# Linear attention and mixture of depths on one core: the first four passes written apart, the order of the later ones changed

## The chip, the core and the metric

One core of a Trainium2 chip. The metric is the device time of one execution in microseconds. The core has five engines with a queue each: PE (TensorE, matmuls and transposes), DVE (VectorE), ACT (ScalarE), POOL (GpSimd) and SP (SyncE, which here only issues DMAs). Each engine takes its instructions in the order in which the kernel writes them, and they wait for one another through semaphores.

## The reference

q, k and v are 8 batches x 8 heads x 576 positions x 64, in float32. With softmax of q over its 64 features and softmax of k over the 576 positions, per head

```
kv  = softmax_seq(k)^T @ v          # 64 x 64
x_h = softmax_feat(q) @ kv          # 576 x 64
```

and the heads side by side make x, 576 x 512 for each batch. Then a mixture of depths: scores are x @ w_gate; the 128 positions with the highest scores of each batch are chosen, and for these alone

```
out[chosen] = x[chosen] + sigmoid(score) * (relu(x[chosen] @ w1) @ w2)   # 512 -> 1024 -> 512
```

Every other row of the output is x.

## The kernel before

A unit is four heads of one batch, so there are 16 units and two to a batch. The kernel's main loop runs over slots `s` = 0 to 19; slot `s` does the attention of unit `s`, prepares unit `s + 1`, and from slot 4 on (`LAG`) also does the MLP of batch `(s - 4) // 2`: its first product (`mlp1`) in the even slots, its second (`mlp2`) in the odd ones, in eight pieces each. Slots 0 to 3 (`EARLY`) have no MLP; filler matmuls (`fill`) stand there instead. The order of all engines' work is written out by hand: what the loop body calls first is first in each engine's queue.

The steps of a unit:
- `load` (L96): k, v and q by two DMAs each on SP's queue, 1.77 MB a unit, into one of three buffers for each (`LD`); a load waits until its buffer has been read.
- `k_exp` (L192) and `q_exp` (L199): exponentials on ScalarE. No maximum is subtracted; a check at the end can start a general version.
- `v_copy` (L202): VectorE copies v beside a column of ones, for the sums of k's softmax.
- `kv_mm` (L212): 40 matmuls of 128 x 64 weights, into a PSUM bank of the pool `tp`. `kv_out` (L221 to L226): reciprocals, the copy of kv into SBUF, and kv times w_gate as one column more.
- `q_t` and `q_t_last` (L235, L244): transposes of exp(q) into `tp` banks; ScalarE (L237) and VectorE (L246) copy them out into `qT`, scaled by the reciprocals of kv.
- `x_mm` (L256): two halves of 40 matmuls of 64 x 64 weights. `x_out` (L269 to L272): VectorE divides by q's sums and writes x and the scores. `x_store` (L277): x goes to the output, on SP's queue.

The steps of a batch, once both units are there: `score`; `score_row` (L305, L308, L310: the scores as a row on every partition, through `tp` banks); five `compare` (L318: each position's rank); `pick` (L338 to L350: a mask of those with ranks below 128, five matmuls on PE that give their indices, and the gather of their rows of x by GpSimd's indirect DMA); `gate`; `turn` (L371, L373: the gathered rows transposed on PE and copied out by ScalarE); `mlp1` (L385, L388), `mlp2` (L395), `finish` (L403, L404: gate and add on VectorE, and the scatter into the output).

PSUM has eight banks: `tp` two, in turn, for q's transposes, kv, score rows and picks; `mm` two, in turn, for fillers, `turn`, `mlp1` and `mlp2`; `x` four, two for each half. A new tile in a bank waits until the one before it there has been read.

In the kernel before, batch 0's `pick` stands in slot 3 and its `turn` in slot 4; in general batch b's pick stands in slot 2b + 3 and its turn at the start of slot 2b + 4:

```
        if chosen is not None:
            pick(chosen)
        if here:
            x_mm(s, 0)
            x_out(s, 0)
```

Of the kernel before, what the change touches and what calls it, by code (L numbers as in the profile page):

```python
# [17 lines left out]
def kernel(  # L18
# [20 lines left out]
    nc = tc.nc  # L39
    B, H, S, D = q.shape  # L40
    DM, F = moe_w1.shape
    P = 128
    R = 5
# [7 lines left out]
    C = D + 2  # L51
# [3 lines left out]
    UP = 2.0 ** 24  # L55
    TINY = 2.0 ** -126
    NV = 5
    WARM = 24
    assert S == 64 * (R + N2) and D == 64 and DM == H * D and DM == 512 and H % 4 == 0
    assert 1 < capacity < S and KF == 8 and NQ == 2  # L60
    assert B * S <= 32 * 256
# [20 lines left out]
    NU = len(units)  # L82
# [115 lines left out]
        qr = raw["q"][u % LD].rearrange("p (i h) r d -> p i r h d", i=2)  # L198
        nc.scalar.activation(out=st["qe", u][:, i], in_=qr[:, i], func=AF.Exp)  # L199

    def v_copy(u):
        nc.vector.tensor_copy(out=v_ones[u % 2][:, :, :, :D], in_=raw["v"][u % LD])  # L202

    def kv_mm(u):

# [19 lines left out]
        nc.vector.tensor_mul(prod, kv[:, :, :D], wg[:, qd])  # L225
        nc.vector.reduce_sum(out=kw[:, :, D + 1], in_=prod, axis=AX.X)  # L226

    def q_t(u, i):

        if i == 0:  # L230
            st["qT", u] = at.tile([P, 2, R, P], F32, tag="qT", name="qT")
        qe = st["qe", u]
        t_ps = bank("tp", 2)
        for r in range(N2):
            nc.tensor.transpose(out=t_ps[:, r * P:(r + 1) * P],  # L235
                                in_=qe[:, i, r].rearrange("p h d -> p (h d)"), identity=ident)
        nc.scalar.activation(out=st["qT", u][:, i, :N2].rearrange("p r c -> p (r c)"), in_=t_ps,  # L237
                             func=AF.Copy, scale=krec[:, u, i:i + 1])
# [10 lines left out]
    def x_mm(u, i):  # L249


        qT = st["qT", u] if i == 0 else st.pop(("qT", u))
        x = ps.tile([P, 2, 512], F32, tag="x", name="x", bufs=2)
        for r in range(R):
            for h, c in ((0, 0), (1, 1), (0, 1), (1, 0)):
                nc.tensor.matmul(out=x[part(c), h, r * C:(r + 1) * C], lhsT=qT[part(h), i, r, part(c)],  # L256
                                 rhs=kv_w[u % 2][part(h), i], start=True, stop=True)
        st["x", u] = x

    xs, sr = {}, {}  # L260

    def x_out(u, i):
        b, qd = units[u]
        if qd == 0 and i == 0:
            xs[b] = xp.tile([P, R, NQ, 2, 2, D], F32, tag="xs", name="xs")
            sr[b] = md.tile([P, NQ * 2, G], F32, tag="sr", name="sr")
        x = st.pop(("x", u))[:, :, :R * C].rearrange("p h (r c) -> p h r c", r=R)
        rec = qrec[:, u, i].rearrange("p (h r) -> p h r", h=2)
        nc.vector.reciprocal(out=rec, in_=x[:, :, :, D])  # L269
        nc.vector.tensor_mul(xs[b][:, :, qd, i].rearrange("p r h d -> p h r d"), x[:, :, :, :D],  # L270
# [248 lines left out]
    v_copy(0)  # L519
    kv_and_exp(0)  # L520
    load(3, "kvq")
    load_w1(0)
    load_w1(1)

    number = None
    for s in range(NU + LAG):

        mlp_b, odd = divmod(s - LAG, 2)
        busy = s >= LAG
        first = busy and odd == 0  # L530
        piece = mlp1 if first else mlp2
        f_next = 0

        def pieces(n):
            nonlocal f_next
            for _ in range(min(n, 8 - f_next) if busy else 0):
                each(piece, mlp_b, f_next)
                f_next += 1

        here = s < NU  # L540
        after = s + 1 < NU
        last = s == NU - 1
        early = s < EARLY
        ends = s // 2 if here and s % 2 == 1 else None
        compared = s // 2 - 1 if s % 2 == 0 and 2 <= s < NU else None
        chosen = (s - 3) // 2 if s % 2 == 1 and 3 <= s < NU else None
        if s == NU:
            chosen = B - 1
        if here:
            q_t(s, 0)  # L550
            q_t_last(s)
        if first:
            each(turn, mlp_b)
        else:
            pieces(1)
        if here:
            q_t(s, 1)
        if early:
            fill(6)
        if compared is not None and early:  # L560
            score_row(compared)
        if after and not early:
            v_copy(s + 1)
        pieces(1)
        if chosen is not None:
            pick(chosen)
        if here:
            x_mm(s, 0)
            x_out(s, 0)
        if compared is not None and not early:  # L570
            score_row(compared)
        if after:
            k_exp(s + 1)
        if compared is not None and early:
            for r in range(R):
                compare(compared, r)
        if after and early:
            v_copy(s + 1)
        pieces(1)
        if here:  # L580
            x_mm(s, 1)
            x_out(s, 1)
            x_store(s)
        if early:
            fill(6)
        if last:
            score(ends)
        pieces(1)
        if after:
            kv_and_exp(s + 1)  # L590
        if early:
            fill(8)
        if s == 0:
            load_w1(2)
            load_w1(3)
        if s + 4 < NU:
            load(s + 4, "kvq")
        if s in (1, 2):
            load_w2(s - 1)
        if compared is not None and not early:  # L600
            for r in range(R):
                compare(compared, r)
        if last:
            score_row(ends)
            for r in range(R):
                compare(ends, r)
        if chosen is not None:
            each(gate, chosen)
        if ends is not None and not last:
            score(ends)  # L610
        pieces(8)
        if busy and odd == 1:
            each(finish, mlp_b)
        if s == NU:
            number = sums_in_range()
# [28 lines left out]
```

## Time and profile before

| | us |
|---|---|
| median of 3 runs | 238.59 (238.51 to 239.07) |
| the profiled execution | 240.16 |
| its span | 238.4 |
| PE busy | 211.9 (89%) |
| DVE busy | 126.7 (53%) |
| ACT busy | 85.9 (36%) |
| POOL busy | 30.8 (13%) |

The rows below come from the profiled execution; its times count from the span's start. PE is the matmuls, PEld the loads of weights, which overlap them. [...] A float32 matmul shows as two instructions, so an `mlp2` piece (one matmul) is "x2" and an `mlp1` piece (four) is "x8". A line of the chain of waits says from when and for how long a piece of work was what the end waited for.

### The profile page before, as it was taken

What the parts mean: (1) busy time and instruction counts of PE and PEld (TensorE: products, weight loads), DVE (VectorE), ACT (ScalarE), POOL (GpSimd) and SP (SyncE); (2) the same over time, 40 slices, a digit from 0 to 9 for tenths busy, and PEclk for the clock granted to TensorE, in tenths of its full rate; (3) what the DMA queues carried; (4) which work ended last, traced back from release to release, by engine and by line L of the source; (5) the groups of instructions that cost most, each with busy time, mean ns of one, the idle gap of its engine ahead of it and who ended that gap; (6) DMA issues with size and microseconds to landing.
All of it is one profiled execution on the core that took longest, in us unless ns stands there. A gap on an engine that the chain in (4) does not pass through costs nothing.

```text
span 238.4 us, 6902 instructions
## 1 busy us (share of the span) xinstructions
PE 211.9 (89%) x2937; PEld 159.4 (67%) x2937; DVE 126.7 (53%) x379; ACT 85.9 (36%) x146; POOL 30.8 (13%) x74
## 2 busy tenths in 40 slices
PE   6977727879999999999999999999999987998980
PEld 2566626769766995599659956896589646947730
DVE  6455385645954495539653774477447666401010
ACT  2456432446333434444435352626163310110200
POOL 5000100120014001300121011201110112101001
PEclk9999986999999999999999999999999998899997
DMA  6999999999958492759485858530413041101001
GB/s 195 314 357 363 388 374 371 376 381 381 381 167 260 179 319 94 242 200 304 138 257 190 258 168 254 206 102 3 143 47 102 1 145 45 44 3 47 1 5 48
DMA packets 39334, 46.79 MB, mean 196 GB/s; under 512 B 2944, under 2 KB 36736, under 8 KB 39296
## 3 DMA queue, kind: packets, MB, share of 16 engines
q1 hardware_dynamic: 36928, 41.36, 51.6%
q0 software_dynamic: 1280, 4.20, 5.2%
q10 hardware_dynamic: 1088, 0.72, 1.1%
q8 instruction: 25, 0.41, 0.7%
q14 instruction: 13, 0.11, 0.1%
HBM read 34.73 MB, written 11.53 MB: 194 GB/s over the span
## 4 chain that ended last, share of the span: by engine, by line
PE 73%; DMA 11%; DVE 5%; ACT 5%; issue 2%; POOL 1%; SPq 0%; POOLq 0%; ACTq 0%
PE mm L385 26%; PE mm L395 23%; DMA q<-in_q_dram 8%; PE x L256 8%; PE tp L212 7%; PE tp L235 5%; DMA xr<-out_dram,idx 3%; ACT qT L237 2%; PE tp L305 2%; DVE junk L318 2%; ACT qe L199 1%; DVE o L403 1%; DVE v_ones L202 1%; PE tp L244 1%; ACT xT L373 0%
## 5 line engine op out<-in xcount | busy, mean ns | idle before, releaser
L385 PE MATMUL mm<-xT,w 128*128 128x128 f32 x512 | 65.3, 284 | 1.6 <-ACT xT L373 1.6
L385 PEld LDWEIGHTS mm<-xT,w 128*128 128x128 f32 x512 | 60.8, 196 | 3.6 <-ACT xT L373 2.4
L395 PE MATMUL mm<-w,hT 128*128 128x512 f32 x128 | 62.1, 607 | 0.0
L318 DVE SCALAR_TENSOR_TENSOR junk<-srow,s,not_before 128x576 bf16<-128x576 f32 x40 | 32.7, 817 | 2.7 <-ACT srow L310 1.5
L395 PEld LDWEIGHTS mm<-w,hT 128*128 128x128 f32 x128 | 21.7, 190 | 16.5 <-issue 15.3
L212 PE MATMUL tp<-v_ones,ke 128*64 128x65 f32 x640 | 23.5, 229 | 9.5 <-DVE qrec L269 8.6
L212 PEld LDWEIGHTS tp<-v_ones,ke 128*64 128x64 f32 x640 | 21.2, 143 | 15.1 <-issue 12.0
L237 ACT ACTIVATE qT<-tp,krec 128x512 f32<-128x512 f32 x32 | 22.0, 687 | 23.9 <-PE tp L235 23.9
L270 DVE TENSOR_TENSOR xs<-x,qrec 128x640 f32<-128x640 f32 x32 | 26.4, 824 | 1.1
L256 PEld LDWEIGHTS x<-kv_w,qT 64*64 64x64 f32 x1280 | 21.5, 133 | 6.7 <-ACT qe L199 3.8
L256 PE MATMUL x<-kv_w,qT 64*64 64x66 f32 x1280 | 25.6, 223 | 0.0
L199 ACT ACTIVATE qe<-q 128x640 f32<-128x640 f32 x32 | 23.6, 736 | 2.7 <-DMA q<-in_q_dram 2.7
L269 DVE RECIPROCAL qrec<-x 128x10 f32<-128x10 f32 x32 | 7.0, 220 | 31.7 <-PE x L256 31.7
L235 PE MATMUL tp<-ident,qe 128*128 128x128 f32 x128 | 19.9, 279 | 2.9 <-ACT qT L237 2.4
L235 PEld LDWEIGHTS tp<-ident,qe 128*128 128x128 f32 x128 | 14.6, 143 | 11.2 <-ACT qT L237 7.9
L350 POOL DMA_INDIRECT xr<-out_dram,idx x8 | 7.9, 992 | 105.3 <-DVE qrec L269 72.6
L403 DVE SCALAR_TENSOR_TENSOR o<-mm,g,xr 128x512 f32<-128x512 f32 x8 | 6.0, 750 | 29.0 <-PE mm L395 29.0
L192 ACT ACTIVATE ke<-k 128x1280 f32<-128x1280 f32 x16 | 20.4, 1272 | 1.8 <-DMA k<-in_k_dram 1.8
L223 ACT COPY kv_w<-tp 128x130 f32<-128x130 f32 x16 | 4.3, 266 | 45.3 <-DVE krec L221 45.3
L388 ACT ACTIVATE hT<-mm 128x512 f32<-128x512 f32 x16 | 9.6, 597 | 29.3 <-PE mm L385 29.3
L404 POOL DMA_INDIRECT out_dram<-o,idx x8 | 11.2, 1397 | 40.4 <-DVE o L403 40.4
L221 DVE RECIPROCAL krec<-tp 128x2 f32<-128x2 f32 x16 | 2.7, 171 | 20.3 <-PE tp L212 20.3
(83 smaller groups left out, 146.9 us busy)
## 6 DMA issues: line engine op xcount, KB each, us to landing
k<-in_k_dram SPq DMA_DIRECT2D x16, 320.0 KB, 5.2
q<-in_q_dram SPq DMA_DIRECT2D x16, 320.0 KB, 6.4
out_dram<-xs SPq DMA_DIRECT2D x16, 320.0 KB, 3.2
v<-in_v_dram SPq DMA_DIRECT2D x15, 320.0 KB, 5.8
k<-in_k_dram SPq DMA_DIRECT2D x16, 256.0 KB, 4.4
q<-in_q_dram SPq DMA_DIRECT2D x16, 256.0 KB, 7.0
out_dram<-xs SPq DMA_DIRECT2D x16, 256.0 KB, 3.7
v<-in_v_dram SPq DMA_DIRECT2D x15, 256.0 KB, 5.3
```

The costliest lines, as they stand in the source:

```text
L192: nc.scalar.activation(out=ke, in_=raw["k"][u % LD], func=AF.Exp)
L199: nc.scalar.activation(out=st["qe", u][:, i], in_=qr[:, i], func=AF.Exp)
L212: nc.tensor.matmul(out=kv[part(h), i], lhsT=ke[:, 2 * i + h, r], rhs=vo[:, 2 * i + h, r], start=(r == 0), stop=(r == N2))
L235: nc.tensor.transpose(out=t_ps[:, r * P:(r + 1) * P], in_=qe[:, i, r].rearrange("p h d -> p (h d)"), identity=ident)
L237: nc.scalar.activation(out=st["qT", u][:, i, :N2].rearrange("p r c -> p (r c)"), in_=t_ps, func=AF.Copy, scale=krec[:, u, i:i + 1])
L256: nc.tensor.matmul(out=x[part(c), h, r * C:(r + 1) * C], lhsT=qT[part(h), i, r, part(c)], rhs=kv_w[u % 2][part(h), i], start=True, stop=True)
L270: nc.vector.tensor_mul(xs[b][:, :, qd, i].rearrange("p r h d -> p h r d"), x[:, :, :, :D], rec.to_broadcast([P, 2, R, D]))
L318: nc.vector.scalar_tensor_tensor(junk, st["srow", b], st["s", b][:, r:r + 1], not_before[:, r], op0=OP.subtract, op1=OP.is_ge, accum_out=s ...
L385: nc.tensor.matmul(out=h_ps[:, f % 4 * m:(f % 4 + 1) * m], lhsT=w1[:, d, f * P:(f + 1) * P], rhs=xT[:, d, :m], start=(d == 0), stop=(d == ...
L388: nc.scalar.activation(out=hT[:, f - 3:f + 1, :m], in_=h_ps[:, :4 * m].rearrange("p (f c) -> p f c", f=4), func=AF.Relu)
L395: nc.tensor.matmul(out=st["y", b, n][:m], lhsT=st["hT", b, n][:, f, :m], rhs=w2[:, f], start=(f == 0), stop=(f == KF - 1))
L404: nc.gpsimd.indirect_dma_start(out=out_rows[:(b + 1) * S], out_offset=bass.IndirectOffsetOnAxis(ap=idx[:m, :1], axis=0), in_=o[:m], in_off ...
```

## The change

- The first four slots leave the main loop and are written as a loop of their own. There the transposes of the second half of q go to an `mm` bank; `k_exp` comes right after them; `v_copy` runs on GpSimd; both halves of x are computed before either is evicted, with fillers around them.
- Batch 0's score row, compares and pick stand in slot 2 instead of slots 2 and 3: the compares ahead of the x matmuls of unit 2, the pick after kv of unit 3, with ten more fillers before it; x of unit 2 is evicted and stored, and kv of unit 3 read, after the pick. Batch 0's gate and turn stand after slot 3.
- w1's four loads are issued in slots 0 and 1 instead of two before slot 0 and two in it; w2's in slots 2 and 3 instead of 1 and 2.
- In the later slots `v_copy` and `k_exp` of the next unit come right after the first transposes; the two halves of x and kv of the next unit follow one another without MLP pieces between; the score row and compares come after that; `turn` of the next batch stands in the odd slot before the last piece of `mlp2`, where the pick of that batch is too.
- 20 warm-up matmuls instead of 24.

```diff
--- before.py
+++ after.py
@@ -55,7 +55,7 @@
     UP = 2.0 ** 24
     TINY = 2.0 ** -126
     NV = 5
-    WARM = 24
+    WARM = 20
     assert S == 64 * (R + N2) and D == 64 and DM == H * D and DM == 512 and H % 4 == 0
     assert 1 < capacity < S and KF == 8 and NQ == 2
     assert B * S <= 32 * 256
@@ -198,8 +198,8 @@
         qr = raw["q"][u % LD].rearrange("p (i h) r d -> p i r h d", i=2)
         nc.scalar.activation(out=st["qe", u][:, i], in_=qr[:, i], func=AF.Exp)
 
-    def v_copy(u):
-        nc.vector.tensor_copy(out=v_ones[u % 2][:, :, :, :D], in_=raw["v"][u % LD])
+    def v_copy(u, engine=nc.vector):
+        engine.tensor_copy(out=v_ones[u % 2][:, :, :, :D], in_=raw["v"][u % LD])
 
     def kv_mm(u):
 
@@ -225,12 +225,12 @@
         nc.vector.tensor_mul(prod, kv[:, :, :D], wg[:, qd])
         nc.vector.reduce_sum(out=kw[:, :, D + 1], in_=prod, axis=AX.X)
 
-    def q_t(u, i):
+    def q_t(u, i, tag="tp"):
 
         if i == 0:
             st["qT", u] = at.tile([P, 2, R, P], F32, tag="qT", name="qT")
         qe = st["qe", u]
-        t_ps = bank("tp", 2)
+        t_ps = bank(tag, 2)
         for r in range(N2):
             nc.tensor.transpose(out=t_ps[:, r * P:(r + 1) * P],
                                 in_=qe[:, i, r].rearrange("p h d -> p (h d)"), identity=ident)
@@ -255,7 +255,7 @@
             for h, c in ((0, 0), (1, 1), (0, 1), (1, 0)):
                 nc.tensor.matmul(out=x[part(c), h, r * C:(r + 1) * C], lhsT=qT[part(h), i, r, part(c)],
                                  rhs=kv_w[u % 2][part(h), i], start=True, stop=True)
-        st["x", u] = x
+        st["x", u, i] = x
 
     xs, sr = {}, {}
 
@@ -264,7 +264,7 @@
         if qd == 0 and i == 0:
             xs[b] = xp.tile([P, R, NQ, 2, 2, D], F32, tag="xs", name="xs")
             sr[b] = md.tile([P, NQ * 2, G], F32, tag="sr", name="sr")
-        x = st.pop(("x", u))[:, :, :R * C].rearrange("p h (r c) -> p h r c", r=R)
+        x = st.pop(("x", u, i))[:, :, :R * C].rearrange("p h (r c) -> p h r c", r=R)
         rec = qrec[:, u, i].rearrange("p (h r) -> p h r", h=2)
         nc.vector.reciprocal(out=rec, in_=x[:, :, :, D])
         nc.vector.tensor_mul(xs[b][:, :, qd, i].rearrange("p r h d -> p h r d"), x[:, :, :, :D],
@@ -519,97 +519,112 @@
     v_copy(0)
     kv_and_exp(0)
     load(3, "kvq")
-    load_w1(0)
-    load_w1(1)
+
+
+    for s in range(EARLY):
+        q_t(s, 0)
+        q_t_last(s)
+        q_t(s, 1, "mm")
+        k_exp(s + 1)
+        v_copy(s + 1, nc.gpsimd)
+        if s == 2:
+            score_row(0)
+            for r in range(R):
+                compare(0, r)
+        fill(6)
+        x_mm(s, 0)
+        x_mm(s, 1)
+        fill(6)
+        if s != 2:
+            x_out(s, 0)
+            x_out(s, 1)
+            x_store(s)
+        if s % 2 == 1:
+            score(s // 2)
+        if s == 2:
+            kv_mm(s + 1)
+            q_exp(s + 1, 0)
+            fill(10)
+            pick(0)
+            x_out(s, 0)
+            x_out(s, 1)
+            x_store(s)
+            kv_out(s + 1)
+            q_exp(s + 1, 1)
+        else:
+            kv_and_exp(s + 1)
+        fill(8)
+        if s == 0:
+            load_w1(0)
+            load_w1(1)
+        elif s == 1:
+            load_w1(2)
+            load_w1(3)
+        load(s + 4, "kvq")
+        if s >= 2:
+            load_w2(s - 2)
+    each(gate, 0)
+    each(turn, 0)
 
     number = None
-    for s in range(NU + LAG):
+    for s in range(EARLY, NU + LAG):
 
         mlp_b, odd = divmod(s - LAG, 2)
-        busy = s >= LAG
-        first = busy and odd == 0
-        piece = mlp1 if first else mlp2
+        piece = mlp2 if odd else mlp1
         f_next = 0
 
         def pieces(n):
             nonlocal f_next
-            for _ in range(min(n, 8 - f_next) if busy else 0):
+            for _ in range(n):
                 each(piece, mlp_b, f_next)
                 f_next += 1
 
         here = s < NU
         after = s + 1 < NU
         last = s == NU - 1
-        early = s < EARLY
-        ends = s // 2 if here and s % 2 == 1 else None
-        compared = s // 2 - 1 if s % 2 == 0 and 2 <= s < NU else None
-        chosen = (s - 3) // 2 if s % 2 == 1 and 3 <= s < NU else None
-        if s == NU:
-            chosen = B - 1
+        ends = s // 2 if here and odd else None
+        compared = s // 2 - 1 if here and not odd else None
+        chosen = (s - 3) // 2 if here and odd else B - 1 if s == NU else None
         if here:
             q_t(s, 0)
             q_t_last(s)
-        if first:
-            each(turn, mlp_b)
-        else:
-            pieces(1)
+        if after:
+            v_copy(s + 1)
+            k_exp(s + 1)
+        pieces(1)
         if here:
             q_t(s, 1)
-        if early:
-            fill(6)
-        if compared is not None and early:
-            score_row(compared)
-        if after and not early:
-            v_copy(s + 1)
         pieces(1)
         if chosen is not None:
             pick(chosen)
         if here:
             x_mm(s, 0)
+            x_mm(s, 1)
             x_out(s, 0)
-        if compared is not None and not early:
+            x_out(s, 1)
+            x_store(s)
+        if last:
+            score(ends)
+        if after:
+            kv_and_exp(s + 1)
+        if s + 4 < NU:
+            load(s + 4, "kvq")
+        pieces(1)
+        if last:
+            compared = ends
+        if compared is not None:
             score_row(compared)
-        if after:
-            k_exp(s + 1)
-        if compared is not None and early:
             for r in range(R):
                 compare(compared, r)
-        if after and early:
-            v_copy(s + 1)
-        pieces(1)
-        if here:
-            x_mm(s, 1)
-            x_out(s, 1)
-            x_store(s)
-        if early:
-            fill(6)
-        if last:
-            score(ends)
-        pieces(1)
-        if after:
-            kv_and_exp(s + 1)
-        if early:
-            fill(8)
-        if s == 0:
-            load_w1(2)
-            load_w1(3)
-        if s + 4 < NU:
-            load(s + 4, "kvq")
-        if s in (1, 2):
-            load_w2(s - 1)
-        if compared is not None and not early:
-            for r in range(R):
-                compare(compared, r)
-        if last:
-            score_row(ends)
-            for r in range(R):
-                compare(ends, r)
         if chosen is not None:
             each(gate, chosen)
         if ends is not None and not last:
             score(ends)
-        pieces(8)
-        if busy and odd == 1:
+        pieces(4)
+        if odd and mlp_b + 1 < B:
+            each(turn, mlp_b + 1)
+        pieces(1)
+        if odd:
             each(finish, mlp_b)
         if s == NU:
             number = sums_in_range()
```

## Rows read from the trace of the kernel before

**Rows 1.** The page's row of DMA rates, in 40 slices of 5.96 us.
```profile
GB/s 195 314 357 363 388 374 371 376 381 381 381 167 260 179 319 94 242 200 304 138 257 190 258 168 254 206 102 3 143 47 102 1 145 45 44 3 47 1 5 48
```

**Rows 2.** Busy time in two stretches: length, PE, PEld, DVE, ACT, POOL, granted clock, DMA.
```profile
30.00:40.00 10.00, 4.73 (x133) 4.39 (x123) 7.29 (x19) 2.49 (x6) 0.00 (x0) 0.68 1.07 375
100.00:120.00 20.00, 19.85 (x337) 16.22 (x338) 12.44 (x33) 8.90 (x15) 2.61 (x2) 1.00 0.67 217
```

**Rows 3.** Timeline of PE, first transposes of slots 1 to 4: start, duration, instruction.
```profile
18.41 0.61 PE L235 MATMUL tp<-ident,qe 128*128 128x128 f32 x4
...
26.60 0.61 PE L235 MATMUL tp<-ident,qe 128*128 128x128 f32 x4
...
40.03 0.79 PE L235 MATMUL tp<-ident,qe 128*128 128x128 f32 x4
...
47.96 0.61 PE L235 MATMUL tp<-ident,qe 128*128 128x128 f32 x4
```

**Rows 4.** Timeline of slot 2: first compare, copy of v, kv, kv's reduce.
```profile
31.68 0.81 DVE L318 SCALAR_TENSOR_TENSOR junk<-srow,s,not_before 128x576 bf16<-128x576 f32 x1
...
35.86 0.82 DVE L202 COPY v_ones<-v 128x1280 f32<-128x1280 f32 x1
...
36.83 2.44 PE L212 MATMUL tp<-v_ones,ke 128*64 128x65 f32 x40 [5.27 <-DVE qrec L269]
...
40.14 0.29 DVE L226 TENSOR_REDUCE kv_w<-prod 128x2 f32<-128x128 f32 x1
```

**Rows 5.** The chain that ended last, 31 to 53 us: start, duration, work.
```profile
31.05 6.38 DMA q<-in_q_dram
...
43.43 6.76 DMA xr<-out_dram,idx
...
51.57 1.16 PE mm L385 x8
```

**Rows 6.** Costs by line and shape: count, busy us, mean ns, idle before.
```profile
L270 DVE TENSOR_TENSOR xs<-x,qrec 128x640 f32<-128x640 f32 x32 | 26.4, 824 | 1.1
L237 ACT ACTIVATE qT<-tp,krec 128x512 f32<-128x512 f32 x32 | 22.0, 687 | 23.9 <-PE tp L235 23.9
L192 ACT ACTIVATE ke<-k 128x1280 f32<-128x1280 f32 x16 | 20.4, 1272 | 1.8 <-DMA k<-in_k_dram 1.8
L403 DVE SCALAR_TENSOR_TENSOR o<-mm,g,xr 128x512 f32<-128x512 f32 x8 | 6.0, 750 | 29.0 <-PE mm L395 29.0
L104 POOL MEMSET q<- 128x256 f32 x2 | 0.6, 304 | 0.0
masks.py:199 POOL TENSOR_SCALAR_AFFINE_SELECT ident<-ident 128x128 f32<-128x128 f32 x1 | 0.3, 291 | 0.1
```

**Rows 7.** The chain that ended last, in slots 6 and 7.
```profile
74.34 0.45 PE tp L235 x4
...
76.27 1.00 PE mm L385 x8
...
80.34 1.09 PE mm L385 x8
...
82.75 4.66 PE mm L385 x40
...
88.06 0.86 PE mm L395 x2
...
90.33 0.74 PE x L256 x40
91.07 1.05 PE mm L395 x2
```

**Rows 8.** Timeline of PE in slot 0: both halves of x in one run.
```profile
13.72 1.40 PE L256 MATMUL x<-kv_w,qT 64*64 64x66 f32 x80
```

**Rows 9.** The chain that ended last, the last two batches' first products.
```profile
200.70 7.98 PE mm L385 x56
...
217.01 7.41 PE mm L385 x64
```

## The prediction

> **What bounds the kernel now.** I read the page's rows by slices first, then the chain that ended last, then the timeline of the early passes, and last the costs by line. The slices [rows 1] show two regimes. Up to about 58 us the DMA moves 357 to 388 GB/s in almost every slice and TensorE has holes: between 30 and 40 us it is busy 4.73 us of 10, at a mean granted clock of 0.68, with the DMA full (share 1.07) [rows 2]. Later, between 100 and 120 us, TensorE is busy 19.85 of 20 us at full clock and the DMA only 0.67 [rows 2]. So late passes cost what TensorE's instructions cost, and early passes cost what a chain of small steps or the transfers cost.
>
> The early passes ("slots") begin with the transposes of q. I take each slot's length from those starts: slot 1 at 18.41, slot 2 at 26.60, slot 3 at 40.03, slot 4 at 47.96 [rows 3]. So slot 1 takes 8.2 us, slot 2 takes 13.4, slot 3 takes 7.9. In slot 2 VectorE does the first output half, then five compares from 31.68 to 35.86, and only then the copy of v that the next kv product waits for; the product starts at 36.83 and runs 2.44 us at the low clock [rows 4]. Then the gather of batch 0 goes out at 43.43, lands 6.76 later, and the first MLP piece starts at 51.57 [rows 5]. That last number is where the dense regime begins.
>
> **The change, part by part.** The sum is against the profiled execution, 240.16 us (span 238.4), which is 1.57 above the median 238.59; I take 1.57 off at the end.
>
> *Early slots.* Three waits go. The second q transposes use a bank of another pool, so they no longer wait for ScalarE's copy out of the first. Both halves of x are computed before anything is evicted, and k's exp stands behind the two copies on ScalarE. The copy of v leaves VectorE, so kv no longer stands behind the first output half. A slot is then: transposes 0.61 [rows 3], two qT copies of 0.69 and one exp of 1.27 in a row on ScalarE (2.65) [rows 6], kv 1.4, fillers about 0.6; with the first transposes ahead this is about 5.3 us. Slot 0 should hand over about 1.1 us earlier (17.3), bounded by q of unit 1; slot 1 takes 5.3 instead of 8.2, so slot 2 starts near 22.6.
>
> Slot 2 keeps the long chain: transposes, ScalarE's two copies and exp, the row of scores copied (about 4.4 us in), five compares 4.2 us (31.68 to 35.86 [rows 4]), the mask and the small steps to the indices about 1.6, so the gather's indices are ready some 10.3 us in, at 33. Now x is evicted after that: twice 0.82 plus two small ones each, 2.4 us in all (the 0.82 from [rows 6]), and kv of unit 3 can only be read after it. That read ends about 0.9 us later (kv product's end 39.27 to the reduce at 40.14 [rows 4]). Slot 3's first transposes want the bank that holds this kv, so slot 2 lasts about 13.6 us, as before, and slot 3 starts at 36.2. So the choice moved ahead gives slot 2 nothing by itself; it takes the gather out of slot 3. Slot 3: 5.3 plus 1.5 for the low clock (2.44 against 1.4 for kv shows the size) makes 6.8, so 43.0.
>
> The gather also waits for the store of slot 1. Queued ahead of and with it on SP: five loads of 1.77 MB, two stores of 0.59 and half of w1 (1.05), 11.1 MB. By the GB/s row [rows 1] times 5.96 us a slice, 11.1 MB have moved at about 33.6 us; the load of unit 4 lands 2.5 us later than this count says in the kernel before (11.5 MB at 34.9, landed at 31.05 + 6.38 = 37.4 [rows 5]). So the store lands at about 36, and the gather 6.76 later [rows 5], at 43. It meets slot 3's end; the cover for it is nil, and each us it is late costs one. Turn at 43.2, three groups of transposes, first piece at 45.0 with 0.45 of transposes still owed, against 51.57 with none owed: **6.1 us** gained. Bounds: 2 (slot 3 keeps its 7.9, gather late by 3 or more) to 8 (no low clock).
>
> The copies on GpSimd: no row shows one. From below, GpSimd's memset does 256 elements in 304 ns, so 1280 in 1.5 us; from above, its select does 128 in 291 ns, so 1280 in 2.9 us [rows 6]; VectorE takes 0.82 [rows 4]. I take 1.6, nearest to the memset, which also just streams. It is hidden by two qT copies and the exp (2.65) if v has landed, and v lands ahead of q; at 2.9 slots 0, 1 and 3 lose 0.3 each. In slot 3 the copy stands behind the gather on GpSimd's queue (36 plus about 1.2), ready at 39, and kv is due at 41: hidden, but uncovered if the gather is issued after 38.
>
> [...]
>
> Four warm-up matmuls less cost and gain nothing: kv of unit 0 then starts sooner, but slot 0 opens with transposes of q, which is loaded last of the three, and these set it anyway (bounds: 0.4 either way).
>
> *w1 and w2 later on SP.* w1's second half is now behind unit 4, w2 behind units 6 and 7. w1 is complete after 12.1 MB, at 36.5 plus 2.5, before the first piece at 45. w2's second half comes after 20.7 MB, which the GB/s row reaches at 59.5, so it lands near 61.5; its first use is in slot 5 at about 63.5. Cover 2 us; cost 0, at worst 2.
>
> *Later slots.* Here a saving is TensorE time. The terms are for a pair (even and odd slot).
> - Odd: an MLP piece (two matmuls) takes 0.86 between transposes and 1.05 after a half of x [rows 7]. Two such switches go: 0.38.
> - Even: eight matmuls after x take 1.09; in the run of 40 they take 4.66/5 = 0.93 [rows 7]. One such switch goes: 0.16.
> - Halves of x side by side: 80 matmuls took 1.40 [rows 8], two times 40 at 0.74 take 1.48 [rows 7]; 0.08 twice: 0.16.
> - The turn leaves the even slot's start: there, 74.34 to 76.27 = 1.93 us hold transposes 0.45, 0.22, 0.45 and the turn 0.45 = 1.57; the rest, 0.36, is waiting on ScalarE [rows 7]. Gone; the turn's own copy is then hidden by the last piece.
> - New: the first MLP1 piece takes the bank of the last MLP2 result, and must wait for VectorE's 0.75 us eviction [rows 6] where only 0.67 of transposes stand between: minus 0.2.
> - New: x next to kv. No row shows this switch. Bounds: 0 (like x after x) and 0.19 (like a piece after x), twice a pair. I take 0.05, nearest to x after x, both being 64-column tiles: minus 0.1.
>
> Sum 0.76 a pair, six pairs: **4.6 us**. On its range: 1.06 without the two new costs, 0.38 less with the dear switch, and another 0.3 less if the mask for the choice comes late. The last is nearly tight: in the even slot the compares now begin behind both halves of x, kv_out and the score copies, about 8.3 us in, end at 12.6, and the mask is ready at 14.75 where TensorE arrives at 14.9. So 0.1 to 1.06 a pair, 0.6 to 6.4 in all.
>
> [...]
>
> *End.* No piece stands between the last x halves, so VectorE has them sooner by about 0.5 (two evictions of about 1.2 now pace it), and two MLP1 pieces instead of one run ahead of the last choice. The 56 matmuls after it took 7.98 us where the same rate as the undisturbed 64 (7.41) gives 6.48 [rows 9]: 1.5 lost to a fallen clock, which may come back if TensorE idles less. The last MLP1 then waits for VectorE's 0.75. I take **0.7**, bounds minus 0.3 and 2.2.
>
> Sum: 240.16 - 6.1 - 4.6 - 0.7 = 228.8; less 1.57: **227.2**.
>
> **Rivals.**
> - *The transfers hold the early stage.* DMA is full to 58 us, so shorter slots only wait elsewhere: the gather lands late or w2 or a unit is missing. For: 375 GB/s throughout [rows 2]. Against: what slot 4 needs is 13.9 MB of the 20.7 moved by 59. The early gain falls to 1: 232.3.
> - *The late stage gives nothing*: switch x to kv dear and mask late, 0.1 a pair: 231.2.
> - *All goes well*: no low clock in slot 3 or at the end, both new costs nil: early 8, late 6.4, end 2: 222.2.
> - *Slower.* In each odd slot the matmuls of the choice stand in TensorE's order ahead of both x halves and kv. If the compares end d later than worked out, TensorE stands for d each pair. The gains are 11.4 us, so above 1.9 us a pair it is slower; at 2.4 (compares starting behind the next unit's second exp and late score copies) it is 241.6. Against: 12.44 us of VectorE work in 20 [rows 2] leave room.
> - *The change doesn't do what it says*: free banks are not free, the early slots keep their lengths, and VectorE's new order eats the late gain: 238.6.
>
> **How the numbers follow.** Forecast 0.58; transfers 0.12; late stage nil 0.12; all well 0.08; slower 0.06; no change 0.04. About 0.3% (0.7 us) is what a measurement of this kernel can tell from no change. So faster 0.90, same 0.04, slower 0.06. The forecast's own range is 224 to 230.5; the 8-in-10 range takes in the transfers' and the late rivals: 222.8 to 233.0.
>
> **What would show it.** After: the start of the first MLP piece near 45 instead of 51.57; slot 2's VectorE order compares, mask, x; the gather issued near 36; copies of v on GpSimd of 1.3 to 2.9 us; a pair of late slots near 23.8 instead of 24.5; no MLP piece right after x; a wait of about 0.2 for the eviction at an even slot's first piece. Wrong would be: a first piece after 49, pairs of 24.5 or more, or TensorE waiting for the mask in each odd slot.

## The result, and the profile after

The changed kernel takes 230.2 us (median of four runs, 228.69 to 230.96) against 238.83 (238.51 to 239.8) on the same chip: ratio 0.9624, 95% interval [0.9567, 0.9681]. The forecast was 227.2 with a range of 222.8 to 233.0: faster, as said, by 3 us less than said. The profiled run (230.25 us, span 228.5) is read below against the 238.4 of before.

The stretches of [rows 2], after: length, PE, PEld, DVE, ACT, POOL, granted clock (as a share of TensorE's full clock), DMA.

```profile
24.00:28.00 4.00, 3.62 (x24) 3.56 (x24) 1.18 (x4) 1.75 (x4) 1.22 (x1) 0.58 1.06 408
30.00:40.00 10.00, 5.46 (x93) 4.52 (x83) 8.05 (x23) 2.37 (x6) 2.43 (x2) 0.74 1.07 381
36.00:47.00 11.00, 9.34 (x161) 8.16 (x159) 6.52 (x24) 4.51 (x8) 3.43 (x7) 0.59 1.07 376
100.00:120.00 20.00, 19.67 (x253) 15.10 (x250) 13.03 (x40) 7.79 (x15) 1.97 (x6) 1.00 0.68 210
```

TensorE is still half empty between 30 and 40 us (5.46 of 10) with the DMA full (1.07), and it is no longer quite full between 100 and 120 (19.67 for 19.85). TensorE's timeline of slots 1 to 4 answers to [rows 3 to 5]; the bracket is idle time before the instruction and what ended it.

```profile
16.68 0.60 PE L235 MATMUL tp<-ident,qe 128*128 128x128 f32 x4
...
20.56 1.27 PE L212 MATMUL tp<-v_ones,ke 128*64 128x65 f32 x36
24.38 0.34 PE L212 MATMUL tp<-v_ones,ke 128*64 128x65 f32 x4 [2.55 <-issue]
...
25.47 1.06 PE L235 MATMUL tp<-ident,qe 128*128 128x128 f32 x4
...
36.48 1.06 PE L235 MATMUL tp<-ident,qe 128*128 128x128 f32 x4
39.20 0.79 PE L244 MATMUL tp<-ident,qe 128*128 128x128 f32 x2 [1.66 <-DVE prod L225]
...
41.41 2.48 PE L256 MATMUL x<-kv_w,qT 64*64 64x66 f32 x80
...
47.98 1.16 PE L385 MATMUL mm<-xT,w 128*128 128x128 f32 x8
```

The first MLP piece starts at 47.98 instead of 51.57. A last group of transposes (0.45) still has to follow it, so the early part gained 3.1 us, not 6.1. Inside the kv product of unit 2 TensorE stops for 2.55 us after 36 of 40 matmuls, and "issue" says that it waited for nothing that the profile shows. After that it runs at a granted clock of 0.58 (24 to 28 us), and slot 2 opens at 25.47 instead of the 22.6 worked out.

From there to slot 15's first transposes (185.39 before, 177.56 after) another 4.7 us are gained (forecast 4.6), and from there to the end 2.1 (53.0 to 50.9; forecast 0.7). 3.1, 4.7 and 2.1 are the 9.9 by which the span fell. A pair of later slots, after:

```profile
71.78 0.60 PE L235 MATMUL tp<-ident,qe 128*128 128x128 f32 x4
72.22 0.38 PE L244 MATMUL tp<-ident,qe 128*128 128x128 f32 x2
72.44 1.06 PE L385 MATMUL mm<-xT,w 128*128 128x128 f32 x8
...
74.75 1.40 PE L256 MATMUL x<-kv_w,qT 64*64 64x66 f32 x80
76.08 1.39 PE L212 MATMUL tp<-v_ones,ke 128*64 128x65 f32 x40
77.40 1.16 PE L385 MATMUL mm<-xT,w 128*128 128x128 f32 x8
...
88.97 0.71 PE L212 MATMUL tp<-v_ones,ke 128*64 128x65 f32 x16 [0.30 <-issue]
...
95.31 0.60 PE L235 MATMUL tp<-ident,qe 128*128 128x128 f32 x4
```

The pair takes 23.53 us (71.78 to 95.31) against 24.54 before (74.17 to 98.71). Neither of the two new costs is there: the first piece starts right behind the transposes, and from x to kv and from kv to the next piece there is no gap (x starts, and kv 1.33 later; kv, and the piece 1.32 later). But in the odd slot TensorE again stops inside kv for no shown reason, after 24 of 40 matmuls. A like row comes back at 112.52, 136.06 and 159.60. With a kv of 1.86 instead of 1.32 it costs 0.54 a pair.

### The profile page after: what moved, and what is told of

Same layout as the page of the kernel before. It is cut to its first block, busy times and chain, and to the rows that moved or that the text cites. A ratio compares the mean times of both kernels' runs of the same rounds, so it can differ in the third digit from the quotient of the medians.

```text
span 228.5 us, 6904 instructions
## 1 busy us (share of the span) xinstructions
PE 207.3 (91%) x2943; PEld 161.2 (71%) x2943; DVE 123.2 (54%) x375; ACT 85.2 (37%) x146; POOL 36.2 (16%) x78
## 3 DMA queue, kind: packets, MB, share of 16 engines
q0 software_dynamic: 1280, 4.20, 5.5%
## 5 line engine op out<-in xcount | busy, mean ns | idle before, releaser
L385 PE MATMUL mm<-xT,w 128*128 128x128 f32 x512 | 62.5, 277 | 0.1
L395 PE MATMUL mm<-w,hT 128*128 128x512 f32 x128 | 61.4, 608 | 0.0
L385 PEld LDWEIGHTS mm<-xT,w 128*128 128x128 f32 x512 | 59.3, 192 | 2.1 <-ACT xT L373 1.7
L395 PEld LDWEIGHTS mm<-w,hT 128*128 128x128 f32 x128 | 22.7, 195 | 18.4 <-issue 17.6
L256 PE MATMUL x<-kv_w,qT 64*64 64x66 f32 x1280 | 24.0, 227 | 0.8 <-issue 0.8
L237 ACT ACTIVATE qT<-tp,krec 128x512 f32<-128x512 f32 x28 | 19.2, 684 | 5.4 <-PE tp L235 5.4
L269 DVE RECIPROCAL qrec<-x 128x10 f32<-128x10 f32 x32 | 7.0, 218 | 23.0 <-PE x L256 21.2
L404 POOL DMA_INDIRECT out_dram<-o,idx x8 | 11.8, 1478 | 47.4 <-DVE o L403 47.4
L235 PEld LDWEIGHTS tp<-ident,qe 128*128 128x128 f32 x112 | 13.6, 147 | 6.4 <-ACT qT L237 3.5
L235 PE MATMUL tp<-ident,qe 128*128 128x128 f32 x112 | 17.8, 283 | 0.1
L373 ACT COPY xT<-mm 128x512 f32<-128x512 f32 x8 | 4.7, 585 | 27.3 <-PE mm L371 27.3
```

Source lines behind the costliest of these rows:

```text
L235: nc.tensor.transpose(out=t_ps[:, r * P:(r + 1) * P], in_=qe[:, i, r].rearrange("p h d -> p (h d)"), identity=ident)
L385: nc.tensor.matmul(out=h_ps[:, f % 4 * m:(f % 4 + 1) * m], lhsT=w1[:, d, f * P:(f + 1) * P], rhs=xT[:, d, :m], start=(d == 0), stop=(d == ...
L395: nc.tensor.matmul(out=st["y", b, n][:m], lhsT=st["hT", b, n][:, f, :m], rhs=w2[:, f], start=(f == 0), stop=(f == KF - 1))
L404: nc.gpsimd.indirect_dma_start(out=out_rows[:(b + 1) * S], out_offset=bass.IndirectOffsetOnAxis(ap=idx[:m, :1], axis=0), in_=o[:m], in_off ...
```

## The experiments

The edits below are shortened; unless another base is named, + is what the run has and - what the changed kernel has in its place.

**The two halves of the change alone.** e1 is the changed kernel with the old loop for the slots after the fourth; e2 has the old first four slots and the new later ones.

```
e1: -    each(turn, 0)
    +        if first: each(turn, mlp_b)      # and all of the old later slots
e2: -        q_t(s, 1, "mm")
    -        v_copy(s + 1, nc.gpsimd)
    +        q_t(s, 1); ... v_copy(s + 1)     # and all of the old early slots
```

> The four early slots are those of the changed kernel, the later slots those of the kernel before (turn at the start of the even slots, MLP pieces between the halves of x). From the two profiles I put the early part at 3.1 us of the 9.9 us of span, the later pairs at 4.7 and the end at 2.1. If the parts simply add up: 3 us faster than before, about 235.5, first MLP piece near 48 us, pairs of later slots at 24.5. Rival: the early gain is only kept because the later slots no longer wait for it (the MLP then finds its gather or w2 late); then under 1.5 us faster, with a wait for a transfer in slots 4 to 7.

> The four early slots and the load order of w1 and w2 of the kernel before, 24 warm-up matmuls, then the later slots of the changed kernel with batch 0's turn ahead of slot 4. If the parts add up: 6.8 us faster than before (4.7 in the pairs, 2.1 at the end), about 232, pairs of later slots at 23.5 instead of 24.5. Rival: the later saving needs the earlier start (its transfers are ahead by then): under 5 us faster.

e1 took 236.33, ratio 0.9896 [0.9852, 0.994]; e2 231.09, ratio 0.9639 [0.9577, 0.9701]. The early slots are worth some 3 us and the later ones some 8. The later ones alone give more than the 6.8 that they give in the whole change (4.7 in the pairs, 2.1 at the end): e2's pair takes 22.98 (78.34 to 101.32) and has no stop. In e1, the early stop stays (2.49 us at 22.43).

**What stops TensorE early.** Three edits. e3 computes the same filler columns in wider matmuls, which takes 63 matmuls out of TensorE's list; e4 leaves the list alone and issues the loads from unit 3 on later, so that the DMA is quieter around 20 us; e5 has the wide fillers in slots 2 and 3 only, behind the stop.

```
e3: -        for _ in range(n):
    -            nc.tensor.matmul(out=junk_ps[:, :P], ..., rhs=ones_b[:, :P], ...)
    +        for c in range(0, n * P, 4 * P):
    +            w = min(4 * P, n * P - c)
    +            nc.tensor.matmul(out=junk_ps[:, :w], ..., rhs=ones_b[:, :w], ...)
e4: -    load(3, "kvq")
    +        if s == 1:
    +            load(3, "kvq"); load(4, "kvq"); load_w1(0..3)
    +        elif s == 2: load(5, "kvq")
    +        elif s == 3: load(6, "kvq"); load(7, "kvq"); load_w2(0); load_w2(1)
e5: +        fill(6, s >= 2)                  # wide only there
```

> The changed kernel with the same filler columns in a quarter of the instructions (512 columns in one matmul instead of four of 128), so that TensorE reaches a given place in its instruction list some 22 matmuls later. In the changed kernel TensorE stops 2.55 us inside the kv product of unit 2, after 36 of its 40 matmuls, with no wait that the profile shows; the kernel before stops there 0.95 us, after 33, with four warm-up matmuls more ahead: the same place in the list. Theory 1 (TensorE ran out of instructions at a fixed place in its list): the stop moves to the fillers or x matmuls of slot 2, slot 2 opens near 22.5 instead of 25.5, the first MLP piece comes 1.5 to 2.5 us sooner (about 46), total 228 to 229. Theory 2 (the stop belongs to that product: its operands, banks or the clock): the stop stays in the kv product of unit 2, total 230 to 230.5.

> The changed kernel with the loads of unit 3 and all later ones, and w1 and w2, issued only after slot 1, so that the DMA has little to do while TensorE is in the kv product of unit 2; TensorE's list is unchanged. Theory 1a (the stop of 2.55 us there is an instruction transfer held up by the full DMA): the stop shrinks to 0.6 us or less, as in the later slots, where stops of 0.3 to 0.4 us without a shown wait stand at DMA shares under 0.9. Theory 1b (it only depends on how fast TensorE eats its list): it stays at 2 us or more. The total is not what is asked, since the loads are late: 232 to 240.

> The changed kernel with the fillers of slots 2 and 3 alone in few wide instructions (35 matmuls fewer before slot 4), those of slots 0 and 1 as they were. Theory: TensorE's list comes in blocks, and it stops where the end of one falls into the run of x, x and kv, which eats about 120 matmuls in 2.7 us. Then the early stop of 2.5 us in the kv product of unit 2 stays where it is, but the stops of 0.3 us inside kv in slots 7, 9, 11 and 13 go away (the place moves 35 matmuls on, past the run's end), and pairs of later slots take 22.98 us, as in the kernel with all fillers wide, instead of 23.53: 227 to 228. Rival (the later stops came from the early delay or from transfers): pairs stay at 23.5, total 230.

e3 took 224.22, ratio 0.9365 [0.9309, 0.9421], 4 us less than the first theory expected; the late stops are gone too. Its kv of unit 2 runs through, and slot 2 opens at 23.23:

```profile
21.47 1.39 PE L212 MATMUL tp<-v_ones,ke 128*64 128x65 f32 x40
22.79 0.60 PE L511 MATMUL mm<-ones_b 128*128 128x512 bf16 x2
23.23 0.60 PE L235 MATMUL tp<-ident,qe 128*128 128x128 f32 x4
```

Stops are not gone for good. They fall on other work: 0.47 us at 19.85 (x of unit 1), 1.37 at 43.62 (kv of unit 4), 1.65 at 51.70 (kv of unit 5). e4, one run of 235.38, has it at the same matmul, 36 of 40, but short (timeline of PE):

```profile
22.00 1.27 PE L212 MATMUL tp<-v_ones,ke 128*64 128x65 f32 x36
23.85 0.34 PE L212 MATMUL tp<-v_ones,ke 128*64 128x65 f32 x4 [0.57 <-issue]
```

Its rates around there are 188 and 220 GB/s, where the changed kernel has 360 and 398. (Its later loads then cost more than that gives.) Of the 1.98 us that the stop is shorter, 1.44 is TensorE coming later, after another stop of 1.23 that ends at 19.87, so the length alone shows little. The transfers themselves are in the trace. The page of after lists 25 of one queue, 16 KB each:

```profile
q8 instruction: 25, 0.41, 0.7%
```

The DMA view of a tenth of a microsecond, 21.8 to 21.9, of after holds the start of one (count, MB, share of 16 engines in the window; 70.2% of 1.6 us is 1.12 us):

```profile
q8 instruction: 1, 0.02, 70.2%
```

It starts as TensorE stops (20.56 + 1.27 = 21.83), and TensorE goes on 1.4 us after its end. In the kernel before, the view of 23.2 to 23.4 has one of 1.15 us:

```profile
q8 instruction: 1, 0.02, 36.0%
```

and TensorE's timeline there is

```profile
23.64 1.18 PE L212 MATMUL tp<-v_ones,ke 128*64 128x65 f32 x33 [1.08 <-DVE qrec L269]
25.76 0.45 PE L212 MATMUL tp<-v_ones,ke 128*64 128x65 f32 x7 [0.95 <-issue]
```

It is the same place in the list (four warm-up matmuls more, three kv matmuls fewer), but kv began late: it waited 1.08 us for VectorE, until 23.64. The transfer began in the last 0.4 us of that wait, and 33 kv matmuls ran on from there. In both kernels TensorE goes on some 2.5 us after the transfer begins; the changed kernel, without that wait, stopped as its transfer began (21.83), and the stop grew from 0.95 to 2.55. Read so, the old wait was part of the transfer's cover.

Over all kernels the early stops stand at the same places in TensorE's list, whatever work falls there: before its 450th, 706th, 963rd, 1218th, 1475th and 1987th instruction as the traces count them (matmuls, weight loads and the queue's own), up to four records off. That is 256 apart, or twice that. TensorE goes on 1.23 to 1.53 us after such a transfer's end in each of 30 stops of 0.2 us or more there; two of them come only in slot 5 (e5 at 65.62, e2 at 69.98). Whether the DMA's load delays the next transfer can be read from when it starts: 1.2 us after TensorE went on at 19.87 in e4, but 3.1 to 4.0 in nine kernels that stop at the same place with the DMA full. One run of e4 is all there is for it, and e7, with 1.9 at a full DMA, fits less well.

e5 took 230.96, ratio 0.9651 [0.9576, 0.9727], and missed what I expected. The early stop stayed, as it should, but so did the late ones, at the same kv matmul although 35 matmuls fewer stand ahead of them (timeline of PE):

```profile
24.83 0.34 PE L212 MATMUL tp<-v_ones,ke 128*64 128x65 f32 x4 [2.22 <-issue]
...
88.78 0.71 PE L212 MATMUL tp<-v_ones,ke 128*64 128x65 f32 x16 [0.32 <-issue]
```

So the late stops are not tied to such a place. They are of another kind, too. TensorE's x and VectorE's reading of its second half (L269), first in the changed kernel, then in e12, which is e3's kernel once more (below) and whose x starts at 85.61:

```profile
86.42 1.40 PE L256 MATMUL x<-kv_w,qT 64*64 64x66 f32 x80
89.06 0.22 DVE L269 RECIPROCAL qrec<-x 128x10 f32<-128x10 f32 x1 [0.60 <-PE x L256]
```

```profile
87.56 0.21 DVE L269 RECIPROCAL qrec<-x 128x10 f32<-128x10 f32 x1
```

In e12 VectorE reads x 0.55 us after the end of x's row and waits for nothing. In the changed kernel it gets x 1.24 us after, just when TensorE goes on (88.97), although the trace has 24 matmuls of kv as issued behind x by then. So x's results were late, and that is not a lack of instructions. This wait of 0.59 to 0.65 us stands in slots 7, 9, 11, 13 and 15 of the changed kernel, e5, e6 and e7, and in none of these slots in e2, e3, e4 and e9 to e12.

**Single parts, in the kernel with wide fillers (e3).** e6 puts the copies of v back on VectorE, e7 the second q transposes back into the tp banks, e8 the MLP pieces back between the halves of x and kv.

```
e6: -        v_copy(s + 1, nc.gpsimd)
    +        v_copy(s + 1)
e7: -        q_t(s, 1, "mm")
    +        q_t(s, 1)
e8:          x_mm(s, 0)
    +        x_out(s, 0)                      # moved up
    +        pieces(1)
             x_mm(s, 1)
    +        pieces(1)
    ...
    -        pieces(4)
    +        pieces(2)
```

> All fillers wide, and the copies of v in the first four slots on VectorE instead of GpSimd, at the same place in the order; TensorE's list is unchanged. If the copy on GpSimd is worth something by itself: VectorE's copy waits for v (which lands late in slots 0 to 2) and holds up the first evictions or compares behind it, 0.3 to 0.8 us a slot, 225.5 to 227. Rival: the place in the order did it, not the engine (0.82 us on VectorE against 1.25 on GpSimd, both hidden by ScalarE's row of 2.65 us): within 0.7 us of the kernel with wide fillers, 223.5 to 225.

> All fillers wide, and the second q transposes of the first four slots back in the two banks they share with the first ones and kv, so that they wait for ScalarE's copy out again; TensorE's list is unchanged. If that bank is worth what the prediction assumed: 0.4 to 0.8 us a slot on the first qT copies, of which slots 2 and 3 count in full, 225.5 to 227. Rival: the transposes' wait is covered by ScalarE's row of copies and exp, within 0.7 us, 223.5 to 225.

> All fillers wide, and in the later slots an MLP piece again between the two halves of x and one between the second half and kv (with two pieces fewer later on). The pairs of later slots are 22.98 us with wide fillers against 24.54 before, a saving of 1.56. If the switches between small and full tiles carry it (0.19 after each half in the odd slot, 0.16 in the even one, 0.08 for each x run): pairs of 23.6 to 23.8, total 228 to 229.5. Rival: the turn's new place and the halves' earlier evictions carry it: pairs under 23.2, total 224.5 to 226.

e6 took 227.95, ratio 0.9499 [0.9411, 0.9586], and e7 227.96, 0.9519 [0.9445, 0.9592]. Their first MLP pieces start at 46.09 and 46.24, against e3's 45.97: for the early slots the copy on GpSimd is worth nothing that can be told, and the other bank at most 0.3 (e12, the same kernel as e3, has 46.13). Both runs lie outside the two ranges expected. Nearly all of the 3.2 and 3.7 us that they take more than e3, by the ratios, comes later: both have the late stops, and pairs of 23.5. What these two parts have to do with the late stops is open. e7:

```profile
85.75 0.92 PE L212 MATMUL tp<-v_ones,ke 128*64 128x65 f32 x24
87.01 0.70 PE L212 MATMUL tp<-v_ones,ke 128*64 128x65 f32 x16 [0.33 <-issue]
```

e8 took 238.69, ratio 0.9985 [0.995, 1.0019], 9 us above what I expected; all of the gain is gone. Its pair takes 25.56, and its odd slot is

```profile
87.54 0.28 PE L342 MATMUL tp<-vals,hit 128*128 128x5 bf16 x5 [1.30 <-DVE hit L338]
87.75 0.81 PE L256 MATMUL x<-kv_w,qT 64*64 64x66 f32 x40
88.49 1.12 PE L395 MATMUL mm<-w,hT 128*128 128x512 f32 x2
```

1.30 of the 2.58 is TensorE waiting for the mask of the choice, because the pieces push the score row, and with it VectorE's compares, 2.3 us back in the slot before; the rest, 1.28, I put down to the switches (a piece behind a half of x takes 1.09 and 1.06 here, 0.2 more than in a run), of which I had forecast 0.70 for these pieces. The first is the mechanism of the "slower" rival: real, and avoided in the changed kernel because x and kv come first.

**The choice, the turn, the order in slot 2.** Also in the kernel with wide fillers, on one chip, with e3 again beside them as e12. e9 puts the first batch's choice back into slot 3; e10 puts the turn back to the even slot's start; e11 reads kv of unit 3 before x of unit 2 is evicted, and has all of w1 behind slot 1's store.

```
e9:  +        if s == 3: pick(0)              # and no special order in slot 2
e10: +        if not odd and mlp_b > 0: each(turn, mlp_b)
     -        if odd and mlp_b + 1 < B: each(turn, mlp_b + 1)
e11:          if s == 2: ... pick(0)
     +            kv_out(s + 1)
              x_out(s, 0); x_out(s, 1); x_store(s)
     -            kv_out(s + 1)
     ...
     +        if s == 1: load_w1(0..3)        # none in slot 0
```

> The wide-fill kernel once more, unchanged, beside the three others. If the missing stops of 0.3 us inside kv of the later slots are a property of that kernel: 223 to 225.5 again and pairs of 22.98 us. If they come and go with something outside the kernel's lists: 226.5 to 228.5 and pairs of 23.5 us, as the two kernels with the same list for TensorE had them.

> The wide-fill kernel, but the first batch's choice (its last reduce, the pick and the gather) stands in slot 3 again and slot 2's x_out, x_store and kv_and_exp come straight behind the compares. Theory (the choice ahead is worth its time): the gather moves from 36.8 to about 39 to 41 us, the turn and the first MLP piece follow, from 45.97 to 47 to 49, so 225.5 to 227.5. Rival (the choice only pushed x_out of slot 2 and kv_out of slot 3 back by the same 2 us): the first MLP piece within 0.5 us of 45.97 and the time 223 to 225.

> The wide-fill kernel, but the gathered rows are turned at the start of the even slots again, behind the last q transposes. Theory (the turn there costs TensorE a switch of its own): 0.28 to 0.36 us in each of six pairs, a pair from 22.98 to 23.3 us, so 225.9 to 226.4. Rival (the turn is free at either place): pairs within 0.1 us of 22.98 and the time 223.5 to 224.7.

> The wide-fill kernel, but in slot 2 kv_out of slot 3 stands ahead of x_out of slot 2, and the four loads of w1 all stand in slot 1. Theory (VectorE's order holds slot 3: its last q transposes wait 1.70 us for the product by VectorE): that wait goes, the gather lands a little earlier, the first MLP piece starts at about 44 instead of 45.97, so 221.5 to 223. Rival (the gather and TensorE's stop inside kv of slot 4, 1.37 us, set the place of the first MLP piece): it starts at 45.5 to 46.5 and the time is 223.5 to 225.

e12 took 225.14, ratio 0.939 [0.9306, 0.9474], with pairs of 22.98 and no late stop: that these are missing belongs to that kernel, on two chips. Its timeline of PE:

```profile
36.76 0.79 PE L244 MATMUL tp<-ident,qe 128*128 128x128 f32 x2 [1.70 <-DVE prod L225]
...
43.78 0.57 PE L212 MATMUL tp<-v_ones,ke 128*64 128x65 f32 x13 [1.35 <-issue]
...
46.13 1.16 PE L385 MATMUL mm<-xT,w 128*128 128x128 f32 x8
...
85.61 1.40 PE L256 MATMUL x<-kv_w,qT 64*64 64x66 f32 x80
86.94 1.39 PE L212 MATMUL tp<-v_ones,ke 128*64 128x65 f32 x40
88.26 4.56 PE L395 MATMUL mm<-w,hT 128*128 128x512 f32 x10
```

e9 took 224.24, ratio 0.9346 [0.9251, 0.9442]. By the four times of each the mean is 0.9 us below e12's, plus or minus 1.4, so the choice ahead is worth nothing that can be seen. GpSimd's timeline of e9 and of e12 gives the reason:

```profile
38.17 1.17 POOL L350 DMA_INDIRECT xr<-out_dram,idx  x1 [3.34 <-DVE no L348]
```

```profile
37.56 1.17 POOL L350 DMA_INDIRECT xr<-out_dram,idx  x1 [11.86 <-DMA k<-in_k_dram]
```

e12's indices are done at 33.8 (VectorE, L347 and L348), but its gather goes out at 37.56, behind a transfer: of what it needs, only slot 1's store is a transfer. In e9 the indices themselves come last, and the gather is 0.6 later.

e11 moves that store ahead, and there the gather goes out at once (GpSimd, then TensorE):

```profile
34.43 1.18 POOL L350 DMA_INDIRECT xr<-out_dram,idx  x1 [8.57 <-DVE krec L221]
```

```profile
42.56 0.57 PE L212 MATMUL tp<-v_ones,ke 128*64 128x65 f32 x13 [1.81 <-issue]
...
44.91 1.16 PE L385 MATMUL mm<-xT,w 128*128 128x128 f32 x8
```

The wait of 1.70 for the product is gone too, and the first MLP piece starts 1.2 earlier, of the 2 expected; the stop inside kv of unit 4 grew to 1.81 and is now what comes last. e11 took 223.19, ratio 0.9331 [0.924, 0.9422], on average 1.6 us below e12 (0.4 to 2.8). Its median is the lowest of all.

e10 took 229.97, ratio 0.9596 [0.9513, 0.9678], 4.8 us above e12 (4.0 to 5.7), where I expected some 2 us above the wide-filler kernel (225.9 to 226.4). Its pairs take 23.91; the rows of one:

```profile
69.70 0.60 PE L371 MATMUL mm<-ident,xr 128*128 128x128 f32 x4
70.98 1.16 PE L385 MATMUL mm<-xT,w 128*128 128x128 f32 x8 [0.68 <-ACT xT L373]
```

My edit left a piece right behind the turn, where the kernel before had the second q transposes; so ScalarE's copy of the turned rows stands bare, 0.68 of the 0.93. As a price of the turn's old place the run says little; it shows what its copy costs uncovered.

## Why the prediction was right, and where it was off

The direction and the two places of the gain were right; each of the three terms was off.

- *Early slots, 6.1 forecast, 3.1 measured.* The step that failed is "slot 1 takes 5.3 instead of 8.2, so slot 2 starts near 22.6". I counted waits for engines and for data, and no supply of instructions, although the kernel before had a stop of 0.95 at that place. Slot 1 took 8.79, of which 2.55 are the stop; the fillers, which I put at 0.6, took about 2.0 (0.69, 0.44 and 0.83). The sum also had ScalarE's row as what kv comes behind, 3.3 us into the slot; TensorE's own transposes, fillers and x filled 3.88 without a wait (16.68 to 20.56). The rest of the chain came as forecast: slot 2 opens 2.9 us later than worked out, the first piece 3.0. Without that stop (e3) slot 2 opens at 23.23 and the first piece starts at 45.97, near the 22.6 and 45.0.
- *Slot 2 as long as before* held in its sum and not in its boundary. The first transposes did not wait for kv's bank (36.48); the last ones did (39.20, 13.7 after the slot's start, for 13.6 forecast). The choice moved ahead was worth nothing (e9): as worked out, the gather waited for slot 1's store (37.41; forecast 36), and what the move exposed was that kv is read behind two evictions. e11 shows that the gain was there, once store and kv come first.
- *The low clock in slot 3* was too small a term, 1.5: from start to start x took 2.41 us where 1.33 is usual and kv 1.57 for 1.32, and the transposes and fillers from 39.20 on some 1.2 more, together 2.5. The granted clock was 0.59 from 36 to 47 us.
- *Copies of v* took 1.25 us on GpSimd, below my lower bound of 1.5, and hidden.
- *Later slots, 4.6 forecast, 4.7 measured*: right by two errors that cancel. Without stops (e12, 22.98) a pair gains 1.56, not 0.76. In the even slot the pieces gain 0.39 (0.16 forecast), the turn's wait 0.41 (0.36), x 0.16 (0.08) and the score row 0.06; in the odd slot the pieces 0.40 (0.38) and x 0.15 (0.08). The two new costs, 0.2 and 0.1, are nil. The stops then take 0.54 back, and two of 0.40 in x of slot 5 another 0.8 once (63.62 and 64.36). That the switch from x to kv would be dear, as the rival had it, no run shows: kv starts 1.33 us after x and the next piece 1.32 after kv (74.75, 76.08 and 77.40).
- *End, 0.7 forecast, 2.1 measured*, inside its bounds, and that is luck too. The fallen clock met the tail of batch 6's second product, 4.71 for 8 matmuls (granted 0.75 from 186.2 to 190.8), and no longer its successor: 48 matmuls after the choice took 5.60, the undisturbed rate (1.00 from 194.1 to 199.7), where 56 took 7.98 [rows 9] (0.79 from 200.7 to 208.7). TensorE's idle time there is one wait of 2.15 us instead of three of 0.97, 0.68 and 0.95. But the late x of slot 15 (VectorE waits 0.60 at 183.21) stands ahead of that wait. In e12, which has none, the wait is 1.45, the 8 matmuls take 3.60, and the end takes 49.0 us (174.51 to 223.5) against 53.0, a gain of 4.0.
- *The rivals.* "Transfers hold the early stage" is not what happened to data; at the stop of 2.55 it is a transfer of instructions that stands there (1.12 us from 21.8 on, ended 1.4 us before TensorE goes on). "All goes well" (222.2) is about what e11 reaches.

What stays open is the late stops. They are in the changed kernel, e5, e6 and e7, and not in e2, e3, e4 and e9 to e12. TensorE's list isn't it: e4 has that of the changed kernel, and e6 that of e3. Nor have they the early stops' lag: in the changed kernel they end 4.2, 0.7 and 0.2 us after an instruction transfer's end, and once 0.2 before it. VectorE's wait for x says that x's results are late there, not the instructions; what holds them up was not found. Stops inside kv never appear where pieces stand between x and kv in the later slots (before, e1, e8).

## What to carry to other kernels

When you take a wait off a dense engine, ask what ran under it: here an instruction transfer of 1.12 us, which no engine's row lists (it stands in a DMA queue, q8); the stop of 2.55 at it shows only as "issue" inside a run of matmuls. While the DMA is full (1.06 and 1.07 in the stretches above), fewer and wider instructions can help as much as a better order: e3 changes only the fillers, and its first MLP piece starts 2.0 us sooner. Its ratio is 0.9365 for 0.9624, but much of the rest of that goes with the late stops, whose cause is open. Where an engine stops, look at who reads its results: VectorE's wait for x tells the two kinds of stop apart. A step moved ahead is worth something only if its last input is moved too (e9, e11), and a step put elsewhere needs the cover that its follower had (e10).

## What the runs showed of the hardware, unexpected

- TensorE stops for 0.2 to 2.55 us at places some 256 instructions apart, and goes on 1.23 to 1.53 us after the end of a 16 KB instruction transfer (of 1.12 us at the stop in the changed kernel, 1.15 in the kernel before).
- In the late stops the results of x reach VectorE 1.24 us after the end of x's row instead of at most 0.55 (the changed kernel, e12), while matmuls behind x are recorded as issued.
- Switching between 64-row tiles in x, 128-row ones in kv and full matmuls costs next to nothing in the run x, x, kv, piece: x 1.33 and kv 1.32 as elsewhere, and the `mlp1` piece behind kv 1.00 where a piece in a run takes 0.89 (e12). A piece behind a half of x costs 0.2 more each (e8: 1.09 and 1.06).
- A copy of 128 x 1280 f32 takes 1.25 us on GpSimd and 0.82 on VectorE [rows 4].
